# Attention, dense FFN and routed experts in one kernel: how the last two token blocks get their second FFN weight, and which queue asks for the first expert's weights

## The chip, the cores and the metric

The kernel runs on one core of a Trainium2 chip. The metric is the device time of one execution in microseconds (us), lower is better. The kernel before takes 1498.35 us, the median of 3 runs (1492.18 to 1498.37).

## The reference

Three parts follow each other on 4608 tokens of width 512: pooled attention, a dense FFN with a piecewise quadratic activation, and eight routed experts of which each token visits one.

```python
# attention: keys and values averaged over groups of 8 positions
attn = softmax(scale * q @ k_p.T); x = attn @ v_p          # -> [4608, 512]
# dense FFN
h = x @ w_in                                               # [4608, 2048]
g = where(h >= 1, h, where(h <= -1, 0, (h + 1) ** 2 / 4))
x = g @ w_out                                              # w_out [2048, 512]
# routed experts, top 1 of 8
expert = argmax(x @ w_gate); gate = max of softmax
out = gate * (relu(x @ w1[expert]) @ w2[expert])           # w1 [8, 512, 1024], w2 [8, 1024, 512]
```

## The kernel before, in words

Matrix products that need the accuracy are done in three matmuls each: both operands are held as a large part (`hi`, rounded to fp32r) and a rest (`lo`), and hi·hi, hi·lo and lo·hi are added in PSUM. A tensor is split by one Copy on ScalarE (ACT), which writes `hi`, and one subtract on VectorE (DVE), which writes `lo`.

The 36 token tiles of 128 form ten blocks, `BLK = [3, 4, 4, 4, 4, 4, 4, 4, 3, 2]`. The dense FFN is one list of 160 steps `g = 16 * j + m`: block `j`, and chunk `m` of 128 of the 2048 hidden columns. For step g, `f1` makes the hidden chunk (12 matmuls with the block's tokens as columns: 512, 384 or 256) and its activation, and `f2` multiplies it by row chunk m of `w_out` (3 matmuls of 512 columns per token tile). `f1` runs two steps ahead (`AHEAD = 2`): loop turn g issues `f1` of step g + 2, then `f2` of step g, and in two slots between and behind them the attention work for the next block, the routing of the block before and small preparations. Everything is issued in the order in which it is written (a manual schedule), and each engine works through its queue in that order.

The activation of one step is a chain between two engines. DVE clips the PSUM bank (line L535), ACT squares (L536), DVE takes the larger into the bank (L546), ACT copies out the hi part (L547), DVE subtracts to get the lo part (L557). The clipped value lives in one buffer `FR`, the banks `ps[0]` and `ps[1]` alternate, so `f1` of step g + 2 waits for L557 of step g. `f2` of step g reads both parts, and w_out's chunk in `WO[:, g % 4]`.

The split of `w_out` is made once, in block 1: there a chunk comes as fp32 (`load_32`, L509), ACT and DVE split it into `WO` (L512 and the subtract in `low_part`, L233), and the pair of parts is stored to the DRAM buffer `wo_d`. From block 2 on `load_out` (L520) fetches the finished pair from there, 512 KB for each step, requested on ACT's queue right behind L547; it is requested three turns ahead of the `f2` that reads it.

While the last two blocks run, the weights of the expert with the most tokens are fetched too: `load_first(i)`, eight requests of 512 KB into the staging areas `ST1` and `ST2` (in tile `AT`, which the attention has used before), at fixed slots `LF`, on ACT's queue (L761 and L763). At slots of the last block they are split on the chip (`cvt1`, Copy L978), the first tokens of that expert are transposed (`q_tx`, L872 to L876), and `f1e` and `f2e` (L908 to L925) start that expert behind the last block.

Routing of a finished block: DVE transposes its output (L594), PE makes logits (L602, L608), DVE finds places (L620 to L647), SP stores the rows (L648), and POOL scatters the token numbers into `perm_d`, 4 bytes per token, one indirect DMA for each tile (L655). Each scatter waits for the one before. At the end POOL reads a part of the table back (L741), DVE turns it into floats (L747) and PE transposes it (L752).

Of the kernel before, what the change touches and what calls it, by code (L numbers as in the profile page):

```python
# [12 lines left out]
ACTF = mybir.ActivationFunctionType  # L13
# [3 lines left out]
ACT = mybir.EngineType.Activation  # L17
DVE = mybir.EngineType.DVE
POOL = mybir.EngineType.Pool
SP = mybir.EngineType.SP  # L20
# [3 lines left out]
def attention_ffn_routed_experts_kernel(  # L24
# [12 lines left out]
    nc = tc.nc  # L37
# [3 lines left out]
    NE, _, EF = w1.shape  # L41
# [3 lines left out]
    KF = DFF // 128  # L45
# [16 lines left out]
    NB = len(blocks)  # L62
# [7 lines left out]
    w32_d = dram.tile([KF, 128, DM], F32, name="w32_d")  # L70
# [6 lines left out]
    def r32(ap):  # L77
        return ap.bitcast(F32)
# [3 lines left out]
    WO = sb.tile([128, 4, 2, DM], F32R, name="WO")  # L82
# [14 lines left out]
    def at(o, n, p=128):  # L97
        return AT[0:p, o:o + n]

    def fx(o, n):  # L100
        return FX[:, o:o + n]
# [19 lines left out]
    WOF = [fx(512 + 512 * i, 512) for i in range(4)]  # L121
    DFI = [fx(2560 + 512 * i, 512) for i in range(3)]

    EH = fx(512, 1024)
    XG = [fx(2560 + ROW * i, ROW) for i in range(3)] + [fx(2044, ROW)]

    def wi(m, lo, c):
        o = m * 1024 + lo * 512 + c * 128
        return W[:, o:o + 128]
# [49 lines left out]
    FSR = sb.tile([128, 1], I32, name="FSR")  # L179
# [52 lines left out]
    def low_part(lo, x, hi, eng=nc.gpsimd):  # L232
        eng.tensor_tensor(out=lo, in0=x, in1=r32(hi), op=ALU.subtract)  # L233
# [3 lines left out]
    def mix(n=1):  # L237
        for _ in range(min(n, len(pend))):
            pend.popleft()()
# [268 lines left out]
    def load_32(m):  # L508
        nc.scalar.dma_start(out=WOF[m % 4], in_=w32_d[m])  # L509

    def split_out(m):
        nc.scalar.activation(out=WO[:, m % 4, 0], in_=WOF[m % 4], func=ACTF.Copy)  # L512

    def split_low(m):
        low_part(WO[:, m % 4, 1], WOF[m % 4], WO[:, m % 4, 0], nc.vector)
        nc.sync.dma_start(out=r32(wo_d[m]), in_=r32(WO[:, m % 4]))

    def load_out(g):

        nc.scalar.dma_start(out=r32(WO[:, g % 4]), in_=r32(wo_d[g % KF]))  # L520

    def f1(j, m):
        g = j * KF + m
        n = blocks[j][1] * 128
        o = ps[m % 2][:, 0:n]
        for c in range(KD):
            xh, xl = XT[:, j % 2, 0, c, 0:n], XT[:, j % 2, 1, c, 0:n]
            nc.tensor.matmul(o, wi(m, 0, c), xh, start=(c == 0), stop=False)  # L528
            nc.tensor.matmul(o, wi(m, 0, c), xl, start=False, stop=False)  # L529
            nc.tensor.matmul(o, wi(m, 1, c), xh, start=False, stop=(c == KD - 1))  # L530
        r = (JK if j == 0 and m % 2 else FR)[:, 0:n]
        gh, gl = FG[:, g % (AHEAD + 1), 0, 0:n], FG[:, g % (AHEAD + 1), 1, 0:n]


        nc.vector.tensor_scalar(r, o, -1.0, 1.0, op0=ALU.max, op1=ALU.min)  # L535
        nc.scalar.activation(out=r, in_=r, func=ACTF.Square, scale=0.5, bias=half)  # L536
        mix()

        def larger():
            if j == 0:  # L540

                nc.vector.tensor_tensor(out=G32[m % 3], in0=r, in1=o, op=ALU.max)
                if m == KF - 1:
                    load_32(0)
                return
            nc.vector.tensor_tensor(out=o, in0=r, in1=o, op=ALU.max)  # L546
            nc.scalar.activation(out=gh, in_=o, func=ACTF.Copy)  # L547
            if j == 1:
                split_out(m)
                if m + 1 < KF:  # L550
                    load_32(m + 1)
            if g + 1 >= 2 * KF and g + 1 < len(steps):
                load_out(g + 1)
            later.append(lower)

        def lower():
            nc.vector.tensor_tensor(out=gl, in0=o, in1=r32(gh), op=ALU.subtract)  # L557
            if j == 1:
                split_low(m)
        later.append(larger)  # L560

    def f2(j, m):
# [136 lines left out]
    def e1(lo):  # L699
        return W[:, lo * 4096:(lo + 1) * 4096].rearrange("p (c f) -> p c f", c=KD)  # L700
# [4 lines left out]
    ST1 = at(0, 4096).rearrange("p (c f) -> p c f", c=KD)  # L705
    ST2 = at(4096, 4096).rearrange("p (c f) -> p c f", c=KE)
# [47 lines left out]

    def load_first(i):
        if not first:
            first.append(nc.values_load(FSR[0:1, 0:1], engines=[ACT], min_val=0, max_val=NE - 1))
        src = (w1, w2)[i // 4][bass.ds(first[0], 1)].rearrange("o (c p) f -> p (o c) f", p=128)

        if i < 4:  # L760
            nc.scalar.dma_start(out=ST1[:, i:i + 1], in_=src[:, i:i + 1])  # L761
        else:
            nc.scalar.dma_start(out=ST2[:, 2 * i - 8:2 * i - 6], in_=src[:, 2 * i - 8:2 * i - 6])  # L763

    first = []

# [181 lines left out]
    def u_h(j, hf):  # L948
        o = ps[hf]
        x = XR[j % 4]  # L950
        for c in range(KD):
# [4 lines left out]
            nc.tensor.matmul(o, x[:, 1, cs], e1(0)[:, c, fs], start=False, stop=(c == KD - 1))  # L956
        nc.scalar.activation(out=EH[:, hf * 512:(hf + 1) * 512], in_=o, func=ACTF.Relu)

    def u_th(hb, hf, pb):
        for i in range(4):  # L960
            c = 4 * hf + i
            nc.tensor.transpose(pb[:, i * 128:(i + 1) * 128], EH[:, c * 128:(c + 1) * 128],
                                ident)
# [59 lines left out]
    with tc.manual_schedule():  # L1023
# [62 lines left out]
        steps = [(j, m) for j in range(NB) for m in range(KF)]  # L1086
# [14 lines left out]
        def slot(j, s):  # L1101
# [15 lines left out]
            for i in range(8):  # L1117
                if 32 * (j - NB + 2) + s == LF[i]:
                    load_first(i)
# [28 lines left out]
        for m in range(AHEAD):  # L1148
            f1(0, m)
            flush()  # L1150
        for g, (j, m) in enumerate(steps):
# [19 lines left out]
            if g + AHEAD < len(steps):  # L1171
                f1(*steps[g + AHEAD])
            else:
                f1e(0, g + AHEAD - len(steps))
# [192 lines left out]
```

## Time and profile before

| what | before |
|---|---|
| median of 3 runs | 1498.35 us |
| the profiled execution | 1499.88 us, span of its instructions 1497.6 us |
| PE (TensorE matmul) busy | 1441.0 us, 96% of the span |
| DVE, ACT, POOL busy | 789.6, 462.9, 215.1 us (53%, 31%, 14%) |
| moved by DMA | 177.65 MB, mean 119 GB/s |

PE is busy nearly all the time, so a change that leaves its matmuls alone counts by the waits of PE that it removes or makes. Transfers are requested on three queues, ACT's, SP's and POOL's, and run on the same 16 DMA engines. In the rows below, times are us from the start of the span, and the last two blocks run from about 895 to 1035 us. ACTq rows are requests on ACT's queue.

### The profile page before, as it was taken

How to read it: one execution, taken by the hardware profiler on the slowest of the kernel's cores; microseconds unless marked ns; L12 is line 12 of the kernel's file. 1: busy time of each engine (PE TensorE's matmuls, PEld its weight loads, DVE VectorE, ACT ScalarE, POOL GpSimd, SP SyncE). 2: the span in 40 equal slices, each digit the busy share in tenths (PEclk: the TensorE clock that was granted, in tenths of full speed). 3: DMA queues.
4: the chain of work that ended last, by engine and by line, in shares of the span. 5: the costliest groups of instructions: out<-in, count | busy, mean ns of one | idle time of the engine just before them, and what ended most of it. 6: DMA issues, size and time to landing. Idle time of an engine off the chain costs nothing.

```text
span 1497.6 us, 20434 instructions
## 1 busy us (share of the span) xinstructions
PE 1441.0 (96%) x7703; PEld 1165.8 (78%) x7703; DVE 789.6 (53%) x1569; ACT 462.9 (31%) x861; POOL 215.1 (14%) x230
## 2 busy tenths in 40 slices
PE   6899999999999999999999999978999999999997
PEld 5666777778888778788878888867878888888786
DVE  4689887646756655756745546444522222212426
ACT  5344433333333332333333233233111111111324
POOL 3152000001000001010010011002222220111112
PEclk8899999999999999999999999999999999999999
DMA  8575558348458465465374374983331110110414
GB/s 233 165 226 158 179 161 186 104 109 125 126 113 124 122 115 102 141 118 120 120 98 115 103 92 144 155 232 72 112 122 57 57 57 22 43 50 30 140 50 148
DMA packets 106522, 177.65 MB, mean 119 GB/s; under 512 B 48450, under 2 KB 56789, under 8 KB 106400
## 3 DMA queue, kind: packets, MB, share of 16 engines
q10 hardware_dynamic: 22688, 75.77, 24.2%
q1 hardware_dynamic: 76144, 80.00, 19.3%
q0 software_dynamic: 7568, 20.33, 4.3%
q8 instruction: 67, 1.10, 0.4%
q14 instruction: 55, 0.45, 0.1%
HBM read 167.17 MB, written 32.49 MB: 133 GB/s over the span
## 4 chain that ended last, share of the span: by engine, by line
PE 76%; DMA 7%; issue 7%; DVE 7%; ACT 1%; POOL 1%; SPq 1%; ACTq 0%; another core or an unknown queue 0%; POOLq 0%; DVEq 0%
PE ps L528 8%; PE ps L571 8%; PE ps L529 8%; PE ps L530 8%; PE ps L573 7%; PE ps L572 7%; PE ps L908 3%; PE ps L909 3%; PE ps L910 3%; PE ps L923 3%; PE ps L924 3%; PE ps L925 3%; PE ps L357 2%; PE ps L302 2%; PE ps L344 2%
## 5 line engine op out<-in xcount | busy, mean ns | idle before, releaser
L528 PE MATMUL ps<-XT,W 128*128 128x512 f32 (+2 forms) x640 | 250.9, 392 | 0.0
L529 PE MATMUL ps<-XT,W 128*128 128x512 f32 (+2 forms) x640 | 238.1, 372 | 1.6 <-DVE XT L363 1.6
L530 PE MATMUL ps<-XT,W 128*128 128x512 f32 (+2 forms) x640 | 237.7, 371 | 0.0
L571 PE MATMUL ps<-WO,FG 128*128 128x512 f32 x528 | 218.2, 413 | 11.1 <-DMA WO<-wo_d 7.2
L536 ACT ACTIVATE FX<-FX,half 128x512 f32<-128x512 f32 (+2 forms) x152 | 104.0, 684 | 401.7 <-DVE FX L535 398.6
L572 PE MATMUL ps<-WO,FG 128*128 128x512 f32 x528 | 207.8, 394 | 0.0
L573 PE MATMUL ps<-WO,FG 128*128 128x512 f32 x528 | 207.8, 393 | 0.0
L535 DVE TENSOR_SCALAR FX<-ps 128x512 f32<-128x512 f32 (+2 forms) x152 | 96.4, 634 | 156.7 <-PE ps L530 156.5
L914 DVE SCALAR_TENSOR_TENSOR FG<-ps,FG 128x512 fp32r<-128x512 f32 (+1 forms) x64 | 43.2, 674 | 221.3 <-ACT FG L913 221.3
L528 PEld LDWEIGHTS ps<-XT,W 128*128 128x128 f32 x640 | 121.7, 190 | 22.6 <-issue 4.5
L529 PEld LDWEIGHTS ps<-XT,W 128*128 128x128 f32 x640 | 122.0, 191 | 19.0 <-DVE XT L363 2.3
L530 PEld LDWEIGHTS ps<-XT,W 128*128 128x128 f32 x640 | 121.5, 190 | 19.5
L571 PEld LDWEIGHTS ps<-WO,FG 128*128 128x128 f32 x528 | 99.6, 189 | 34.8 <-issue 5.3
L546 DVE TENSOR_TENSOR ps<-FX,ps 128x512 f32<-128x512 f32 (+2 forms) x144 | 92.9, 645 | 55.1 <-ACT FX L536 55.1
L547 ACT ACTIVATE FG<-ps 128x512 fp32r<-128x512 f32 (+2 forms) x144 | 80.9, 562 | 123.6 <-DVE ps L546 113.3
L913 ACT ACTIVATE FG<-ps 128x512 fp32r<-128x512 f32 (+1 forms) x64 | 37.4, 584 | 259.5 <-PE ps L910 258.9
L573 PEld LDWEIGHTS ps<-WO,FG 128*128 128x128 f32 x528 | 99.6, 189 | 22.9
L572 PEld LDWEIGHTS ps<-WO,FG 128*128 128x128 f32 x528 | 99.9, 189 | 17.0
L336 POOL TENSOR_TENSOR AT<-AT,ssm 128x576 f32<-128x576 f32 x36 | 41.4, 1151 | 481.1 <-DVE ssm L329 473.2
L557 DVE TENSOR_TENSOR FG<-ps,FG 128x512 fp32r<-128x512 f32 (+2 forms) x144 | 91.9, 638 | 34.8 <-ACT FG L547 34.4
L923 PE MATMUL ps<-W,FG 128*128 128x512 f32 x248 | 99.2, 400 | 0.0
L908 PE MATMUL ps<-XT,W 128*128 128x512 f32 (+1 forms) x256 | 98.4, 384 | 0.0
(238 smaller groups left out, 2317.9 us busy)
## 6 DMA issues: line engine op xcount, KB each, us to landing
WO<-wo_d ACTq DMA_DIRECT2D x128, 512.0 KB
AT<-in_moe_w_dram SPq DMA_DIRECT2D x10, 2048.0 KB
AT<-in_moe_w_dram SPq DMA_DIRECT2D x14, 1024.0 KB
AT<-in_v_dram SPq DMA_DIRECT2D x60, 144.0 KB
AT<-in_q_dram SPq DMA_DIRECT2D x32, 256.0 KB
wo_d<-WO SPq DMA_DIRECT2D x16, 512.0 KB
AT<-in_k_dram SPq DMA_DIRECT2D x56, 144.0 KB
yrow_d<-Y SPq DMA_DIRECT2D x7, 1032.0 KB
```

Source lines behind the costliest of these rows:

```text
L528: nc.tensor.matmul(o, wi(m, 0, c), xh, start=(c == 0), stop=False)
L529: nc.tensor.matmul(o, wi(m, 0, c), xl, start=False, stop=False)
L530: nc.tensor.matmul(o, wi(m, 1, c), xh, start=False, stop=(c == KD - 1))
L535: nc.vector.tensor_scalar(r, o, -1.0, 1.0, op0=ALU.max, op1=ALU.min)
L536: nc.scalar.activation(out=r, in_=r, func=ACTF.Square, scale=0.5, bias=half)
L546: nc.vector.tensor_tensor(out=o, in0=r, in1=o, op=ALU.max)
L557: nc.vector.tensor_tensor(out=gl, in0=o, in1=r32(gh), op=ALU.subtract)
L571: nc.tensor.matmul(o, gh, WO[:, g % 4, 0], start=(m == 0), stop=False)
L572: nc.tensor.matmul(o, gh, WO[:, g % 4, 1], start=False, stop=False)
L573: nc.tensor.matmul(o, gl, WO[:, g % 4, 0], start=False, stop=(m == KF - 1))
L908: nc.tensor.matmul(o, e1(0)[:, c, ms], xh, start=(c == 0), stop=False)
L923: nc.tensor.matmul(o, gh, e2(0)[:, m], start=(m == 0), stop=False)
```

## The change

Two edits. In the last two blocks (steps 128 to 159, `S0 = 128`) `wo_d` is no longer read. A step's chunk comes as fp32 from `w32_d`, 256 KB, into one of three buffers `WL` in tile `FX`, requested on ACT's queue five turns ahead of its `f2`; two turns later ACT copies the hi part into `WO` and DVE subtracts for the lo part, both behind the activation of the step that is made then. And `load_first` issues on SP's queue instead of ACT's.

```diff
+    WL = [fx(512, 512), fx(1024, 512), fx(2044, 512)]
...
+    S0 = (NB - 2) * KF
+
+    def load_last(g):
+        if S0 <= g < len(steps):
+            nc.scalar.dma_start(out=WL[g % 3], in_=w32_d[g % KF])
+
+    def split_last(g):
+        nc.scalar.activation(out=WO[:, g % 4, 0], in_=WL[g % 3], func=ACTF.Copy)
+
+    def split_last_low(g):
+        low_part(WO[:, g % 4, 1], WL[g % 3], WO[:, g % 4, 0], nc.vector)
...
-            if g + 1 >= 2 * KF and g + 1 < len(steps):
+            if 2 * KF <= g + 1 < S0:
                 load_out(g + 1)
+            load_last(g + 3)
+            if S0 <= g + 1 < len(steps):
+                split_last(g + 1)
             later.append(lower)
...
             nc.vector.tensor_tensor(out=gl, in0=o, in1=r32(gh), op=ALU.subtract)
             if j == 1:
                 split_low(m)
+            if S0 <= g + 1 < len(steps):
+                split_last_low(g + 1)
...
-            first.append(nc.values_load(FSR[0:1, 0:1], engines=[ACT], min_val=0, max_val=NE - 1))
+            first.append(nc.values_load(FSR[0:1, 0:1], engines=[SP], min_val=0, max_val=NE - 1))
...
-            nc.scalar.dma_start(out=ST1[:, i:i + 1], in_=src[:, i:i + 1])
+            nc.sync.dma_start(out=ST1[:, i:i + 1], in_=src[:, i:i + 1])
...
-            nc.scalar.dma_start(out=ST2[:, 2 * i - 8:2 * i - 6], in_=src[:, 2 * i - 8:2 * i - 6])
+            nc.sync.dma_start(out=ST2[:, 2 * i - 8:2 * i - 6], in_=src[:, 2 * i - 8:2 * i - 6])
```

The lines of the changed file stand 13 lower from L536 to L557 (L535 is L548, L536 is L549, L546 is L559, L547 is L560; L557 is L573, 16 lower) and 18 lower behind; L233 is L234.

ACT's queue in the last block, two turns in a row (steps 150 and 151), before; FG is the hidden chunk, FX the tile of the clipped value, AT the staging area, and the DMA rows are requests:

```order
L536 ACTIVATE FX<-FX,half 128x256
L547 ACTIVATE FG<-ps_67 128x256
L520 DMA WO<-wo_d 128x1024
L536 ACTIVATE FX<-FX,half 128x256
L547 ACTIVATE FG<-ps_68 128x256
L520 DMA WO<-wo_d 128x1024
L763 ISA
L763 DMA AT<-in_moe_w_dram 128x2x512
```

The same place of the changed kernel:

```order
L549 ACTIVATE FX<-FX,half 128x256
L560 ACTIVATE FG<-ps_67 128x256
L523 DMA FX<-w_d 128x512
L526 ACTIVATE WO<-FX 128x512
L549 ACTIVATE FX<-FX,half 128x256
L560 ACTIVATE FG<-ps_68 128x256
L523 DMA FX<-w_d 128x512
L526 ACTIVATE WO<-FX 128x512
```

The request is half as large, the expert's request is gone from this queue, and a Copy of 512 columns (L526) stands between L560 of one step and L549 of the next.

DVE's queue over the same two steps, before:

```order
L535 TENSOR_SCALAR FX<-ps_67 128x256
L546 TENSOR_TENSOR ps_67<-FX,ps_67 128x256
L557 TENSOR_TENSOR FG<-ps_67,FG 128x256
L535 TENSOR_SCALAR FX<-ps_68 128x256
L546 TENSOR_TENSOR ps_68<-FX,ps_68 128x256
L557 TENSOR_TENSOR FG<-ps_68,FG 128x256
```

And in the changed kernel:

```order
L548 TENSOR_SCALAR FX<-ps_67 128x256
L559 TENSOR_TENSOR ps_67<-FX,ps_67 128x256
L573 TENSOR_TENSOR FG<-ps_67,FG 128x256
L234 TENSOR_TENSOR WO<-FX,WO 128x512
L548 TENSOR_SCALAR FX<-ps_68 128x256
L559 TENSOR_TENSOR ps_68<-FX,ps_68 128x256
L573 TENSOR_TENSOR FG<-ps_68,FG 128x256
L234 TENSOR_TENSOR WO<-FX,WO 128x512
```

A subtract of 512 columns now stands between the end of one step's activation and the clip of the next.

SP's queue behind the last loads of the attention (q, k, v into AT), before; `yrow_d` is the store of a block's rows, the last three of blocks 7, 8 and 9 among them, and TB the table of the experts' part:

```order
L206 DMA AT<-in_q_dram 128x8x64 x3
L648 DMA yrow_d<-Y 128x4x516 x2
L648 DMA yrow_d<-Y 128x3x516
L648 DMA yrow_d<-Y 128x2x516
L1013 TENSOR_LOAD TB
```

And in the changed kernel, where FSR holds the number of the first expert:

```order
L666 DMA yrow_d<-Y 128x4x516 x2
L775 TENSOR_LOAD FSR
...
L779 DMA AT<-in_moe_w_dram 128x1024
...
L781 DMA AT<-in_moe_w_dram 128x2x512
L781 ISA
L781 DMA AT<-in_moe_w_dram 128x2x512
L666 DMA yrow_d<-Y 128x3x516
L781 ISA
L781 DMA AT<-in_moe_w_dram 128x2x512
L781 ISA
L781 DMA AT<-in_moe_w_dram 128x2x512
L666 DMA yrow_d<-Y 128x2x516
```

The eight requests stand on SP now, six of them directly behind the row store of block 7 and two behind that of block 8.

## Rows read from the trace of the kernel before

**Rows 1.** Two stretches: length; PE, PEld, DVE, ACT, POOL busy (count); PE clock; DMA; GB/s

```profile
895.00:965.00 70.00, 69.87 (x409) 61.15 (x408) 36.99 (x98) 22.26 (x43) 9.00 (x10) 1.00 0.63 135
965.00:1035.00 70.00, 58.29 (x366) 51.07 (x365) 31.20 (x83) 23.48 (x47) 9.02 (x7) 0.95 0.78 196
```

**Rows 2.** Timeline, ACT's queue at the start of the last block (start, us, instruction)

```profile
970.81 4.43 ACTq L761 DMA_DIRECT2D AT<-in_moe_w_dram  x1
975.28 1.09 ACT L580 ACTIVATE Y<-ps 128x512 f32<-128x512 f32 x2 [4.66 <-issue]
```

**Rows 3.** Timeline of PE: waits for w_out (in brackets: idle before, releaser)

```profile
1003.95 0.77 PE L571 MATMUL ps<-WO,FG 128*128 128x512 f32 x1 [4.30 <-DMA WO<-wo_d]
...
1013.02 0.47 PE L571 MATMUL ps<-WO,FG 128*128 128x512 f32 x1 [1.31 <-DMA WO<-wo_d]
...
1026.98 0.47 PE L571 MATMUL ps<-WO,FG 128*128 128x512 f32 x1 [1.59 <-DMA WO<-wo_d]
```

**Rows 4.** Timeline: ACT's requests of two of these three chunks

```profile
998.86 0.33 ACTq L520 DMA_DIRECT2D WO<-wo_d  x1
...
1017.89 0.33 ACTq L520 DMA_DIRECT2D WO<-wo_d  x1
```

**Rows 5.** Timeline of POOL: the first of block 8's three scatters, the table read

```profile
992.61 0.97 POOL L655 DMA_INDIRECT perm_d<-idt,POSI  x1 [27.48 <-DVE SM L646]
...
1023.76 0.90 POOL L741 DMA_INDIRECT FX<-perm_d,RWM  x1 [5.47 <-PE ps L572]
```

**Rows 6.** Timeline: PE's part of one turn, step 155 on f2

```profile
1017.73 0.28 PE L528 MATMUL ps<-XT,W 128*128 128x256 f32 x1
...
1019.16 0.40 PE L571 MATMUL ps<-WO,FG 128*128 128x512 f32 x1
...
1020.55 0.60 PE L872 MATMUL ps<-ident,FX 128*128 128x128 f32 x4
```

**Rows 7.** Timeline: the activation of step 158, to the clip of 159

```profile
1023.16 0.42 DVE L535 TENSOR_SCALAR FX<-ps 128x256 f32<-128x256 f32 x1
...
1023.61 0.51 ACT L536 ACTIVATE FX<-FX,half 128x256 f32<-128x256 f32 x1 [1.15 <-DVE FX L535]
...
1024.15 0.43 DVE L546 TENSOR_TENSOR ps<-FX,ps 128x256 f32<-128x256 f32 x1 [0.58 <-ACT FX L536]
...
1024.62 0.38 ACT L547 ACTIVATE FG<-ps 128x256 fp32r<-128x256 f32 x1 [0.49 <-DVE ps L546]
...
1025.03 0.42 DVE L557 TENSOR_TENSOR FG<-ps,FG 128x256 fp32r<-128x256 f32 x1 [0.45 <-ACT FG L547]
...
1025.43 0.42 DVE L535 TENSOR_SCALAR FX<-ps 128x256 f32<-128x256 f32 x1
```

**Rows 8.** Timeline of block 1, where chunks are split: DVE and ACT

```profile
197.21 0.68 DVE L233 TENSOR_TENSOR WO<-FX,WO 128x512 fp32r<-128x512 f32 x1
...
201.07 0.60 ACT L547 ACTIVATE FG<-ps 128x512 fp32r<-128x512 f32 x1 [0.28 <-DVE ps L546]
...
201.56 0.62 ACT L512 ACTIVATE WO<-FX 128x512 fp32r<-128x512 f32 x1
```

**Rows 9.** The same columns, from the clip of step 146 to that of 159

```profile
972.21:1025.43 53.22, 43.10 (x282) 37.73 (x282) 24.67 (x70) 18.97 (x37) 7.27 (x6) 0.94 0.81 194
```

**Rows 10.** Groups of DVE instructions in that stretch (busy, mean; idle before)

```profile
L233 DVE TENSOR_TENSOR W<-AT,W 128x1024 fp32r<-128x1024 f32 x2 | 2.5, 1226 | 2.3 <-ACT W L978 2.3
L594 DVE STREAM_TRANSPOSE WG<-Y 128x512 f32<-128x512 f32 x3 | 2.1, 699 | 0.0
L875 DVE TENSOR_TENSOR XT<-ps,XT 128x512 fp32r<-128x512 f32 x3 | 2.1, 692 | 1.7 <-ACT XT L874 1.7
```

**Rows 11.** Timeline of PE and DVE behind the last block

```profile
1028.34 0.22 DVE L747 CAST FX<-FX 32x128 f32<-32x128 int32 x1 [0.55 <-DMA FX<-perm_d,RWM]
1028.45 0.34 PE L908 MATMUL ps<-XT,W 128*128 128x384 f32 x1
...
1032.04 0.24 PE L752 MATMUL ps<-ident,FX 32*128 32x32 f32 x1
```

## The prediction

> **What bounds the kernel now.** I looked first at the busy time by stretch. In block 8 PE is busy for 69.87 of 70 us, so nothing can be won there; in block 9 and what borders it for 58.29 of 70, at a mean granted clock of 0.95 [rows 1]. So this change is worth something in the 70 us around block 9, or nowhere. The waits of PE there have two causes. Three are for a chunk of w_out that had not landed: 4.30, 1.31 and 1.59 us, 7.2 together [rows 3]. The fourth is behind ACT's queue: one request for the expert's weights held ACT for 4.43 us, the evacuation of block 8 stood behind it and began 4.66 us late [rows 2], and the next f2 needs the banks that it empties. With the lower clock behind the two long waits, about 13 us of PE time are lost.
>
> Why the chunks are late is seen from request and use. The chunk that PE took at 1013.02 was requested at 998.86, 14.2 us before; that of 1026.98 at 1017.89, 9.1 us before [rows 3, 4]. That is not their size: the whole stretch moves 196 GB/s [rows 1], at which 512 KB take 2.7 us. Over the same time POOL's three scatters follow each other, from 992.61 to the table read at 1023.76, 10.4 us each [rows 5]. The use at 1013.02 and the end of the second scatter, by this count at 1013.4, fall together; that at 1026.98 comes behind the third.
>
> **The change, part by part.**
>
> *Requests moved to SP.* ACT no longer issues eight requests. Seven of them cost it nothing that shows; the long one goes, and with it the wait of 4.66 us and the slow matmuls behind it: about 5 us at the start of block 9, if nothing takes their place. On SP they stand behind the row store of block 7 and wait only for their staging area, which the attention has left by then, so they come up to 30 us earlier than on ACT. Nobody waits for SP there; what is queued behind them is the row store of block 8 and two of the eight, read at the expert's start at the earliest. I price the earlier traffic at nothing beside the landings below.
>
> *Chunks loaded at half size.* 32 requests of 512 KB become 32 of 256 KB. They are made five turns ahead of their f2 instead of three, but their first reader is now ACT's Copy two turns after the request. A chunk that is late now holds ACT's queue, and with it every activation, instead of PE alone.
>
> *The splits.* 32 Copies and 32 subtracts of 512 columns. Block 1 has both: the Copy 0.62 us, 0.49 us after L547 starts; the subtract 0.68 [rows 8]. By busy time they fit: in the last block's stretch DVE works 24.67 of 53.22 us and ACT 18.97 [rows 9], and 13 subtracts are 8.8. But they don't lie in a free place. The activation is one chain over two queues that are worked through in order. From one clip to the next it takes 0.45 (clip to square), 0.54 (to L546), 0.47 (to L547), 0.41 (to L557) and 0.40 (to the next clip), 2.27 us [rows 7]. In the changed order the Copy stands behind L547 and the subtract behind the Copy, and the next clip behind the subtract: 0.45 + 0.54 + 0.47 + 0.49 (L547 to Copy) + 0.65 (Copy and 0.03 of hand-over) + 0.66 (subtract, with the overlap of 0.02 that rows 7 show) = 3.26 us a turn. PE's own turn is 1.43 us for f1 and 1.39 for f2, 2.82 us [rows 6]. So the chain, which had 0.55 us a turn to spare, becomes 0.44 us longer than PE's turn, and the last block is bound by DVE and ACT together, neither of them busy.
>
> In block 8 the same sum does not bite: tokens are 384 columns and the turn of PE is 70 us over some 15 turns, 4.7 us [rows 1], against 3.26 and some 0.15 for each of the four longer instructions; the cover is 0.8 us a turn, which the attention's last units use up for a few turns, and the two steps of lead hold that. I price block 8 at nothing.
>
> *The sum for the last block*, from the clip of step 146 to that of step 159, 13 turns. Before: 972.21 to 1025.43 [rows 9]. After: the start is 0.4 later, because one subtract stands ahead of it (0.66, less a pause there). 13 turns of 3.26 are 42.4. Other DVE work on the chain: 24.67 busy less 13 x 1.27 for the three steps of the activation (0.42 + 0.43 + 0.42 [rows 7]) leaves 8.2; of it two of the three transposes of L594 (0.7 each) and one of the logits (0.3) stand behind L546, where DVE waits anyway, so 6.5; and DVE's waits for ACT's conversions, 2.3 and 1.7 [rows 10], stay: 10.5. The last term is waiting for landings and for PE's logits. It is bounded by zero (256 KB, requested two turns or 6.5 us ahead) and by the landings of rows 3 and 4: one of 14.2 and two of 9.1 against 6.5 are 12.9. The load on the queues falls by half, and a turn with a conversion is over 4 us long, so I take 2.5, nearer to zero. Sum: 972.6 + 42.4 + 10.5 + 2.5 = 1028.0, the clip of step 159 comes 2.6 us later than before.
>
> PE gives that back. Before, it was behind the chain: f1e began at 1028.45 [rows 11], 3.0 us after the last clip, because of the late chunk. After, f1e needs only the bank that L557 of step 158 frees, 1.80 - 0.83 = 0.97 us ahead of the last clip, so at 1027.1. From there on everything follows as before. **The change gains 1028.45 - 1027.1, 1.3 us.** Against the profiled execution's 1499.88 us that is 1498.6; the median of the three runs, 1498.35, is 1.5 lower than that execution, so I forecast 1497.0. What was lost to transfers is lost to the chain instead.
>
> [...]
>
> **The rivals.**
>
> *B, the splits are hidden.* If a turn stays with PE (the Copy and subtract find room, or my 3.26 is too long), all four waits and the slow matmuls go, 13 us. The next limit is then the chain of scatters: the first is issued at 992.61, the table is read and on DVE at 1028.34, and PE transposes it at 1032.04 [rows 5, 11]. The first scatter would move up by the 5 us lost ahead of it, the table to 1023.5, so PE's transpose comes 8 us earlier and not 13: 1490. If scatters go faster with fewer bytes beside them, up to 1486. For it: both engines have idle time. Against it: the order puts both instructions in the one cycle.
>
> *C, late landings on ACT's queue, slower than before.* The waiting term is all that is needed: the chain has 3.9 us to give (1.3 + 2.5) before the change costs time. Three scatters, each catching one request at its middle, give about 2.6 us each by the 9.1 us landing, 7.8 together, and one more for the scatters of block 7 that run into this block, 10.4: a loss of 6.6, 1505. If the 14.2 us come back once, 5 more. For it: the rows above. Against it: half the bytes, and 2 MB of the expert's weights are moved out of this stretch.
>
> *D, neither edit shows*, because PE catches the evacuation late for another reason and landings decide as before: 1498.
>
> **How the numbers follow.** A (the chain takes over, 1.3 us gained, 1493 to 1501 with the bounds of its terms) 0.58; B 0.23; C 0.14; D 0.05. The range that leaves out no more than 2 in 10 runs from B's middle to below C's: 1488.5 to 1504. Half a per cent, 7.5 us, is about what a measurement can tell here, as the three runs of before lie 6 us apart (1492.18 to 1498.37). Faster by more than that is most of B and a little of the rest: 0.20. Slower is a part of C: 0.10. Same: 0.70.
>
> **What the profile after would show.** Right: no wait at the start of block 9 and no request over 1 us on ACT; PE's waits in block 9 many and short, released by DVE and ACT instead of transfers, 8 to 13 us in all; clips at least 3.2 us apart in turns with no other work; the subtract's wait for the Copy in every turn. B: clips 2.8 us apart, and a wait of L747 or L752 for the table. C: waits of L526 for WL of several us. The forecast fails if the split's Copy or subtract is much quicker here than in block 1, or if landings cost over 4 us.

## The result: 0.8% slower

The changed kernel takes 1510.4 us, the median of 5 runs (1508.27 to 1513.28); in the same session the kernel before takes 1498.37 (5 runs). The ratio is 1.0078, 95% interval 1.0053 to 1.0102; timed again later it was 1511.14 us, 1.0083 (1.0058 to 1.0108). The profiled execution took 1508.75 us, its instructions span 1507.0 us (before: 1499.88 and 1497.6). The forecast of 1497.0 us and its range up to 1504 are missed, on the side of rival C. In this text a late chunk is one that ACT or PE stands and waits for, and the times in the lines are read from one execution each.

The two stretches of [rows 1] in the changed kernel, with the same columns:

```profile
895.00:965.00 70.00, 68.61 (x399) 59.77 (x397) 44.59 (x111) 29.07 (x56) 7.92 (x8) 1.00 0.57 125
965.00:1035.00 70.00, 54.77 (x338) 47.39 (x337) 40.41 (x91) 29.44 (x56) 10.47 (x8) 0.90 0.42 82
```

The last column is in line with the edits: 82 GB/s in place of 196 around block 9. But PE is busy 3.5 us less there, its granted clock fell from 0.95 to 0.90, and block 8, which had no gap, has one. Where PE, ACT and DVE stood (table of waits: engine, line waited for, releaser; us in total, times, longest; PE from 890 to 1130 us, ACT and DVE to 1050):

```profile
PE ps L541 <- DVE FG L573: 10.4, 4, 4.6
...
ACT WO L526 <- DMA FX<-w_d: 9.1, 5, 3.8
...
DVE WO L234 <- ACT WO L526: 11.3, 13, 4.0
```

PE no longer waits for a transfer: the waits of [rows 3] are gone. The transfers are waited for by ACT, at the Copy of the split (L526), 9.1 us in five waits; DVE waits for ACT, and PE for DVE. This is the sign that the forecast gave for C. The first long one, at the start of block 9, in the timeline:

```profile
962.00 0.33 ACTq L523 DMA_DIRECT2D FX<-w_d  x1
...
967.18 1.10 POOL L673 DMA_INDIRECT perm_d<-idt,POSI  x1 [7.81 <-DMA perm_d<-idt,POSI]
...
973.10 0.63 ACT L526 ACTIVATE WO<-FX 128x512 fp32r<-128x512 f32 x1 [3.77 <-DMA FX<-w_d]
...
976.93 1.07 ACT L598 ACTIVATE Y<-ps 128x512 f32<-128x512 f32 x2
...
977.57 0.50 PE L589 MATMUL ps<-WO,FG 128*128 128x512 f32 x1 [3.98 <-ACT Y L598]
...
978.27 0.41 DVE L548 TENSOR_SCALAR FX<-ps 128x256 f32<-128x256 f32 x1
```

The last scatter of block 7 goes out at 967.18; ACT stands 3.77 us for a chunk that was requested at 962.00, 11.1 us earlier; the evacuation L598 is behind it in the same queue, and PE waits for that 3.98 us (3.8 before). So the 4.66 us of [rows 2] were not removed but exchanged: a chunk in place of a request, on the same queue, in front of the same instruction.

A turn without any other work, DVE and ACT:

```profile
999.59 0.42 DVE L548 TENSOR_SCALAR FX<-ps 128x256 f32<-128x256 f32 x1
1000.04 0.51 ACT L549 ACTIVATE FX<-FX,half 128x256 f32<-128x256 f32 x1 [1.09 <-DVE FX L548]
1000.59 0.43 DVE L559 TENSOR_TENSOR ps<-FX,ps 128x256 f32<-128x256 f32 x1 [0.58 <-ACT FX L549]
1001.11 0.38 ACT L560 ACTIVATE FG<-ps 128x256 fp32r<-128x256 f32 x1 [0.56 <-DVE ps L559]
...
1001.53 0.43 DVE L573 TENSOR_TENSOR FG<-ps,FG 128x256 fp32r<-128x256 f32 x1 [0.51 <-ACT FG L560]
1001.56 0.63 ACT L526 ACTIVATE WO<-FX 128x512 fp32r<-128x512 f32 x1
...
1002.23 0.69 DVE L234 TENSOR_TENSOR WO<-FX,WO 128x512 fp32r<-128x512 f32 x1 [0.27 <-ACT WO L526]
1002.83 0.42 DVE L548 TENSOR_SCALAR FX<-ps 128x256 f32<-128x256 f32 x1
```

From clip to clip 3.24 us, step by step as the forecast put it together from [rows 7, 8]; it said 3.26. The next turn, and what follows from it. The first row is the request of the chunk that is late in it; the last two are the start of f1e and the clip of step 159, which were at 1028.45 and 1025.43 before:

```profile
997.88 0.33 ACTq L523 DMA_DIRECT2D FX<-w_d  x1
...
1007.56 0.63 ACT L526 ACTIVATE WO<-FX 128x512 fp32r<-128x512 f32 x1 [2.82 <-DMA FX<-w_d]
...
1012.72 0.44 PE L541 MATMUL ps<-XT,W 128*128 128x256 f32 x1 [3.96 <-DVE FG L573]
...
1016.18 3.38 DVE L234 TENSOR_TENSOR WO<-FX,WO 128x512 fp32r<-128x512 f32 x1 [0.27 <-ACT WO L526]
...
1016.59 2.41 POOL L234 TENSOR_TENSOR W<-AT,W 128x1024 fp32r<-128x1024 f32 x1
...
1025.24 0.58 PE L541 MATMUL ps<-XT,W 128*128 128x256 f32 x1 [4.65 <-DVE FG L573]
...
1036.49 0.44 PE L926 MATMUL ps<-XT,W 128*128 128x384 f32 x1
...
1037.14 0.42 DVE L548 TENSOR_SCALAR FX<-ps 128x256 f32<-128x256 f32 x1
```

ACT stands 2.82 us for a chunk requested 9.7 us earlier, and PE, which has no turn in hand any more, 3.96 us. Right behind it something comes that the forecast did not know: a subtract of the split lasts 3.38 us in place of 0.69, beside a POOL subtract that makes a part of the expert's weights, and PE waits another 4.65 us. Behind these waits PE's clock is lower for a while: 0.50 is granted from 1013 to 1016, and 0.80 on the mean from 1005 to 1030. f1e begins 8.0 us later than before, and the span ends 9.4 later.

### The profile page after: what moved, and what is told of

Same layout as the page of the kernel before. It is cut to its first block, busy times and chain, and to the rows that moved or that the text cites. A ratio compares the mean times of both kernels' runs of the same rounds, so it can differ in the third digit from the quotient of the medians.

```text
span 1507.0 us, 20498 instructions
## 1 busy us (share of the span) xinstructions
PE 1443.4 (96%) x7703; PEld 1166.4 (77%) x7703; DVE 812.3 (54%) x1601; ACT 481.0 (32%) x893; POOL 215.1 (14%) x230
## 5 line engine op out<-in xcount | busy, mean ns | idle before, releaser
L541 PE MATMUL ps<-XT,W 128*128 128x512 f32 (+2 forms) x640 | 252.7, 395 | 10.5 <-DVE FG L573 10.4
L549 ACT ACTIVATE FX<-FX,half 128x512 f32<-128x512 f32 (+2 forms) x152 | 104.0, 684 | 393.7 <-DVE FX L548 393.4
L548 DVE TENSOR_SCALAR FX<-ps 128x512 f32<-128x512 f32 (+2 forms) x152 | 96.3, 633 | 137.3 <-PE ps L543 137.2
L541 PEld LDWEIGHTS ps<-XT,W 128*128 128x128 f32 x640 | 122.8, 192 | 34.9 <-DVE FG L573 12.5
L543 PEld LDWEIGHTS ps<-XT,W 128*128 128x128 f32 x640 | 123.0, 192 | 19.6
L542 PEld LDWEIGHTS ps<-XT,W 128*128 128x128 f32 x640 | 123.2, 192 | 18.8 <-DVE XT L364 2.3
L559 DVE TENSOR_TENSOR ps<-FX,ps 128x512 f32<-128x512 f32 (+2 forms) x144 | 92.9, 645 | 51.5 <-ACT FX L549 51.5
L560 ACT ACTIVATE FG<-ps 128x512 fp32r<-128x512 f32 (+2 forms) x144 | 81.0, 562 | 122.7 <-DVE ps L559 111.2
L573 DVE TENSOR_TENSOR FG<-ps,FG 128x512 fp32r<-128x512 f32 (+2 forms) x144 | 91.9, 638 | 35.0 <-ACT FG L560 34.6
```

## The experiments

Three theories to begin with. **Theory 1**: late fp32 chunks hold ACT's queue. **Theory 2**: the split lengthens the chain of DVE and ACT beyond PE's turn. **Theory 3**: the expert's traffic, which SP starts earlier, is what makes the chunks late.

### Each edit alone

The requests on SP alone (the last three lines of the diff):

> Only the requests for the first expert's weights are moved to SP; w_out still comes as finished pairs from wo_d. If the move is harmless by itself, the long request on ACT and the 4.66 us wait at the start of block 9 are gone, the waits of PE for w_out chunks (7.2 us before) stay, and the time is 1493 to 1498 us. If the earlier expert traffic is what makes the chunks late (theory 3), the waits of PE for w_out grow to over 12 us, some of them in block 8, and the time is 1500 us or more. No wait of block 9 is released by ACT or DVE for several us, as there are no splits.

1505.26 us, ratio 1.0031 (1.0014 to 1.0049): slower, where the forecast priced this edit as a gain of 5 if nothing took its place. Waits of PE, and one of them in the timeline:

```profile
PE ps L571 <- DMA WO<-wo_d: 12.6, 5, 5.6
```

```profile
957.11 0.76 PE L571 MATMUL ps<-WO,FG 128*128 128x512 f32 x1 [4.46 <-DMA WO<-wo_d]
```

The wait behind the evacuation is gone, but 12.6 us for w_out stand against 7.2, and 4.46 of them in block 8, which had none. Theory 3 is right for this kernel.

The loads and splits alone, the requests on ACT:

> Only the loads as fp32 and the splits; the expert's requests stay on ACT's queue. Theory 1 (late fp32 chunks hold ACT's queue) and theory 2 (the split lengthens the chain of DVE and ACT) both give 1508 to 1516 us, since the cause is all here and the long request of some 4 us on ACT comes back. Theory 3 (the traffic that SP starts earlier makes the chunks late): the waits of L526 fall from 9.1 us to under 3 and the time is within 1496 to 1503 us.

1502.63 us, ratio 1.0030 (1.0010 to 1.0049). In the table of waits:

```profile
ACT WO L526 <- DMA FX<-w_d: 3.2, 4, 1.4
```

3.2 us in place of 9.1 (12.1 when the changed kernel was profiled again, below), just by leaving the expert's requests where they were. Theories 1 and 2, as far as they put the whole loss into this edit, are refuted. By the ratios each edit costs about 4.5 us and both together 11.7; the intervals don't show whether that is more than the sum.

### Only the time of the expert's requests, not their queue

```diff
+    def gate(g):
+        nc.sync.dma_start(out=gate_d, in_=r32(FG[0:1, g % (AHEAD + 1), 1, 0:16]))
...
                 if 32 * (j - NB + 2) + s == LF[i]:
+                    gate(j * KF + s // 2 + 1)
                     load_first(i)
```

> The changed kernel, with the expert's requests still on SP's queue but each behind a 64-byte store on that queue that reads the hidden chunk of the step being made, so that they go out at the steps at which ACT issued them before, and not up to 30 us earlier. If it is the early traffic that makes the chunks late, the waits of L526 fall from 9.1 us to about the 3.2 of the run with the requests on ACT, and the time is 1499 to 1504 us. If SP's queue itself does it, whatever the time, the waits stay at 7 us or more and the time at 1507 or more.

1503.70 us, ratio 1.0041 (1.0029 to 1.0054); L526 waits 3.2 us in six waits, the longest 1.5. So the queue does no harm to the chunks; it is the time of the requests. In the changed kernel SP asks for six times 512 KB right behind the row store of block 7, within some 10 us:

```profile
936.88 2.78 SPq L779 DMA_DIRECT2D AT<-in_moe_w_dram  x4
939.86 5.71 SPq L781 DMA_DIRECT2D AT<-in_moe_w_dram  x2
```

The same hold on the kernel before, with w_out as pairs:

> The kernel before with the expert's requests on SP's queue, held there to the steps at which ACT issued them; w_out as pairs. If the early traffic was the whole harm of the move to SP, PE's waits for w_out go from the 12.6 us of the run without the hold back to the 7 of before, the 4.66 us behind ACT's long request stay away, and the time is 1493 to 1497 us. If not, PE still waits 10 us or more for w_out and the time is 1499 us or more: then the long request cost nothing that was to be had.

1503.10 us, ratio 1.0017 (1.0001 to 1.0033). PE waits 8.9 us for w_out, between the two cases; the time is that of the second, nothing is gained. The long request on ACT is gone, and in the same place PE now waits for a late chunk:

```profile
978.29 0.77 PE L572 MATMUL ps<-WO,FG 128*128 128x512 f32 x1 [3.42 <-DMA WO<-wo_d]
```

That the 4.66 us had covered it before is an inference. What this run shows is the requests on another queue, at the same steps, and no gain (1.0017).

### One turn more of lead

```diff
-    WL = [fx(512, 512), fx(1024, 512), fx(2044, 512)]
+    WL = [fx(512, 512), fx(1024, 512), fx(2044, 512), WG[:, 5]]
...
-            load_last(g + 3)
+            load_last(g + 4)
```

> The changed kernel with four WL buffers in place of three, the fourth in tile WG, so that each fp32 chunk is requested one turn (3.2 us in block 9, 4.7 in block 8) earlier. Theory 1: the waits of L526 fall from 9.1 us to under 2, the evacuation behind block 8 is on time, and of the 12 us lost 6 to 9 come back: 1501 to 1504 us. Theory 2: turns stay at 3.25 us, PE waits in every turn of block 9, and no more than the 3 us of the two long waits beyond the chain come back: 1506 to 1509 us.

1500.45 us, ratio 1.0008 (0.9994 to 1.0022). Waits, and the clips of steps 146 and 159 in the timeline:

```profile
ACT WO L526 <- DMA FX<-w_d: 1.8, 1, 1.8
```

```profile
975.87 0.41 DVE L548 TENSOR_SCALAR FX<-ps 128x256 f32<-128x256 f32 x1
...
1030.69 0.42 DVE L548 TENSOR_SCALAR FX<-ps 128x256 f32<-128x256 f32 x1
```

Theory 1: the lead gives back about 10 us of the changed kernel's loss (1.0078 to 1.0008). Some 2.7 of them may be luck, as no subtract of the split is stretched in block 9 in this execution. The chain is unchanged here, and from clip 146 to 159 it takes 54.8 us.

### The subtract behind the next clip

In f1, where DVE waits for ACT's square anyway; the chain no longer has the subtract in it:

```diff
         nc.vector.tensor_scalar(r, o, -1.0, 1.0, op0=ALU.max, op1=ALU.min)
+        if S0 <= g:
+            split_last_low(g)
...
         def lower():
-            if S0 <= g + 1 < len(steps):
-                split_last_low(g + 1)
```

> The changed kernel, with the subtract of a chunk's split moved on DVE from in front of the next clip to behind it, where DVE waits for ACT's square; loads and their lead are as they were. Theory 2: undisturbed turns of block 9 fall from 3.25 us to PE's 2.82 or so, 13 turns give back 5.6 us, with the lower clock that went with PE's waits 6 to 9: 1501 to 1504 us, the L526 waits as they were or longer. Theory 1: PE's waits go on to follow the late chunks (L526 waits 8 to 12 us, since a shorter turn also shortens the lead), 1507 to 1510 us.

1502.45 us, ratio 1.0008 (0.9988 to 1.0028). Waits:

```profile
ACT WO L526 <- DMA FX<-w_d: 12.4, 8, 5.1
```

Theory 2 has its part too: ACT stands for chunks as long as in the changed kernel or longer (12.4 us; 9.1 and 12.1 in that one's two profiles), and yet most of the loss is gone. The reading is that the chain catches up between the waits.

### Both mends

> Both mends at once: four WL buffers (requests one turn earlier) and the subtract behind the next clip. Each alone gave back 8 to 10 of the 12 us. If late chunks and the long chain are two losses that add up, L526 waits under 3 us in all, turns of block 9 come to 2.8 to 2.9 us, PE's waits in block 9 fall under 4 us, and the time is 1490 to 1495 us, faster than before. If they are one loss that either mend removes (a late chunk costs only while the chain has no slack), the time is 1498 to 1501 us.

1493.80 us, ratio 0.9968 (0.9952 to 0.9983): faster than both kernels. Most of the two gains adds up: by the ratios 16.5 us against the changed kernel, where each mend alone gave about 10. A turn in its timeline, from clip to clip:

```profile
991.87 0.41 DVE L548 TENSOR_SCALAR FX<-ps 128x256 f32<-128x256 f32 x1
...
992.23 0.69 DVE L234 TENSOR_TENSOR WO<-WG,WO 128x512 fp32r<-128x512 f32 x1
992.32 0.51 ACT L551 ACTIVATE FX<-FX,half 128x256 f32<-128x256 f32 x1
...
994.14 0.41 DVE L548 TENSOR_SCALAR FX<-ps 128x256 f32<-128x256 f32 x1
...
1021.68 0.33 PE L926 MATMUL ps<-XT,W 128*128 128x384 f32 x1
```

The subtract L234 runs beside the square, and the turn can go down to 2.27 us, the length before the change, which is less than PE's 2.82. The turns are not all 2.8 to 2.9 us as expected: the 13 from clip 146 to 159 take 46.2 us together, against 53.2 before and 58.9 in the changed kernel. f1e begins at 1021.68, 6.8 us earlier than before. L526 waited 3.7 us in this execution, a little more than expected, all of it in block 8, where the chain has room for it.

Two variants of it, with the expert's requests held to the steps of before, and with all eight of them in block 8:

> Both mends (four WL buffers, subtract behind the next clip) and the expert's requests on SP held to the steps of before. If early expert traffic costs anything beyond the lead of the chunks, this is 2 to 4 us faster than the same kernel without the hold; if a turn more of lead covers it, the two agree within 2 us. By the forecast's case B it is 1488 to 1494 us.

> Four WL buffers, the subtract behind the next clip, and all eight expert requests in block 8. If a turn more of lead covers the traffic in block 8 too, this is 0 to 3 us faster than the same kernel with two requests in block 9 (1493.8 us), 1490 to 1494. If the bunch in block 8 gets too large for the lead, L526 waits over 6 us there and the time is 1495 to 1500 us.

1494.68 us, ratio 0.9970 (0.9959 to 0.9982), and 1494.06 us, 0.9957 (0.9941 to 0.9974). The three agree: with a turn more of lead and the subtract moved, it doesn't matter where the traffic lies.

### POOL's subtract beside the split's

The two subtracts of the first expert's weights that POOL makes in block 9 are given to DVE (two, not the four that the expectation names); on the changed kernel, on the one with both mends, and the changed kernel once more beside them:

```diff
-        low_part(e1(1)[:, c], ST1[:, c], e1(0)[:, c], nc.gpsimd if c % 2 else nc.vector)
+        low_part(e1(1)[:, c], ST1[:, c], e1(0)[:, c], nc.vector)
```

> The changed kernel with the first expert's four subtracts on POOL (2.4 us each) made by DVE, where they take 1.23 us. If POOL's instruction is what stretches DVE's subtracts with two operands in SBUF, no subtract of the split lasts over 0.75 us any more, the turn from clip 154 to 155 falls from 6.59 us to 5.2 or less (one subtract of 1.23 may lie in it), and the time is 0 to 3 us less than the changed kernel's, since DVE now has 1.23 us more in two turns of the block. If something else stretches them (the lower clock behind a wait, a landing), the turn stays over 6 us or another subtract is stretched, and the time is 1 to 4 us more.

> The kernel with four WL buffers and the subtract behind the next clip, and the same move from POOL to DVE. If POOL's instruction stretches DVE's, no subtract of the split lasts over 0.75 us; the time is within 2 us of the 1493.8 of the same kernel without the move, since its chain has the room for one stretched subtract. If the stretch cost it anything near 3 us, the time is 1489 to 1491.

> The changed kernel once more, nothing edited: 1508 to 1512 us, ratio 1.006 to 1.010.

1512.17 us, ratio 1.0096 (1.0073 to 1.0119); 1492.76, 0.9968 (0.9955 to 0.9982); 1511.14, 1.0083 (1.0058 to 1.0108). Timed again, the changed kernel once more has a stretched subtract of 3.26 us, and the turn from clip 154 to 155 lasts 6.49 us (6.59 the first time). Without POOL's two, no subtract of the split lasts over 0.69 us from 940 us on, and this turn is 3.90. So POOL's instruction is the cause; but the time did not fall as expected. DVE's 1.23 us now lie in the chain in other turns (that from 153 to 154 is 4.72 us in place of 3.24), and the 13 turns last 59.1 us. With both mends the time is the same with and without the move. That it is not the number of columns shows in the kernel with both mends, at a subtract of 16 columns of the routing:

```profile
1040.61 2.39 POOL L234 TENSOR_TENSOR W<-AT,W 128x1024 fp32r<-128x1024 f32 x1 [8.88 <-ACT W L1001]
...
1040.64 2.39 DVE L659 TENSOR_TENSOR G<-G,ebase 128x16 f32<-128x16 f32 x1
```

It starts 0.03 us behind POOL's and ends with it (1043.03 and 1043.00). The subtract of 3.38 us starts 0.41 us ahead of POOL's by the profile and ends 0.56 us behind it. Why a DVE instruction lasts longer beside POOL's is not shown.

### What holds a chunk: traffic, row store or scatter

All eight expert requests ahead of block 8's row store, so that block 9 has no such traffic:

```diff
-    LF, CV1, QT0 = (24, 26, 28, 30, 33, 36, 39, 42), (13, 15, 18, 21), (17, 20, 23)
+    LF, CV1, QT0 = (24, 26, 28, 30, 33, 36, 37, 38), (13, 15, 18, 21), (17, 20, 23)
```

> The changed kernel with the last two of the expert's eight requests moved in the program ahead of block 8's row store on SP, so that all eight go out in block 8 and none beside the first scatter of block 9. If the bunched expert traffic is what makes a chunk late, the wait of L526 at about 1007 us (2.82 us) falls under 0.5 us and those in block 8 and at its end (6.3 us) grow by 1 to 4. If a scatter in flight is enough, the wait in block 9 stays at 2 us or more. Time 1504 to 1511 us either way.

1507.99 us, ratio 1.0056 (1.0034 to 1.0078). In the timeline:

```profile
997.04 0.97 POOL L673 DMA_INDIRECT perm_d<-idt,POSI  x1 [26.11 <-DVE SM L664]
997.31 0.37 SPq L666 DMA_DIRECT2D yrow_d<-Y  x1
...
1007.60 0.63 ACT L526 ACTIVATE WO<-FX 128x512 fp32r<-128x512 f32 x1 [2.08 <-DMA FX<-w_d]
```

The wait stays at 2.08 us without the traffic. The waits ahead of it, which were expected to grow by 1 to 4 us, are 6.3 us in sum as before; the longest in block 8 is 4.70 us, against 1.48 and 4.01 in the two profiles of the changed kernel. But the row store is requested 0.27 us after the scatter and is a rival to it. Three kernels look at that, all with this order of the expert's requests, in one execution each, so that their rows are read and not their times. Moving the scatters in the program by twelve steps of the routing's list:

> The kernel with all eight expert requests in block 8, and block 8's three scatters issued three turns later (first at about 1007 us in place of 997), with the table read behind them moved too; the row store of block 8 stays at about 997. If a scatter in flight is what holds a chunk's landing, there is no wait of L526 over 0.5 us between 995 us and the first scatter, and one of 1.5 us or more within 10 us behind it. If the row store (774 KB) beside the chunks does it, the wait of 2.08 us stays at about 1007. The table read comes some 10 us later, so the time is not compared.

It told nothing: POOL had nothing to do in between and issued the first scatter at 996.36 all the same; the wait (1.88 us) stood at 1006.74. To hold the scatters, they were then made to read their places from a copy that DVE writes at that step; and in the other kernel the row store was put behind a 64-byte store of the hidden chunk, on SP:

> All eight expert requests in block 8, and block 8's scatters held back some three turns by letting them read their places from a copy that DVE makes at that step; the row store stays at about 997 us. If the scatter in flight holds the landings, no wait of L526 over 0.5 us stands between 995 us and the first scatter, and one of 1.5 us or more stands within 10 us behind it. If the row store does it, the wait of about 2 us stays at 1005 to 1009 us. The table read comes later by as much, so the time is not compared.

> All eight expert requests in block 8, the scatters where they were (first at about 997 us), and the row store of block 8 held back on SP's queue until some five turns later. If the scatter in flight holds the landings, the wait of L526 at 1005 to 1009 us stays at 1.5 us or more. If the row store does it, that wait falls under 0.5 us and one may stand where the row store goes now.

With the scatters held:

```profile
1004.09 0.37 SPq L666 DMA_DIRECT2D yrow_d<-Y  x1
...
1014.08 1.97 POOL L675 DMA_INDIRECT perm_d<-idt,WG  x1 [38.37 <-DVE WG L685]
...
1026.25 0.63 ACT L526 ACTIVATE WO<-FX 128x512 fp32r<-128x512 f32 x1 [2.14 <-DMA FX<-w_d]
```

The DMA engines in two stretches of that execution (columns as in [rows 1]):

```profile
1014.08:1025.00 10.92, 8.87 (x54) 7.10 (x52) 6.30 (x13) 5.38 (x10) 3.88 (x3) 1.00 0.70 24
1025.00:1027.00 2.00, 0.00 (x0) 0.00 (x0) 0.00 (x0) 0.75 (x2) 1.41 (x1) 1.00 0.74 263
```

And with the row store held:

```profile
998.62 0.97 POOL L678 DMA_INDIRECT perm_d<-idt,POSI  x1 [27.46 <-DVE SM L670]
...
1004.75 0.38 SPq L649 DMA_DIRECT2D yrow_d<-Y  x1
...
1009.13 0.63 ACT L527 ACTIVATE WO<-FX 128x512 fp32r<-128x512 f32 x1 [2.02 <-DMA FX<-w_d]
```

The wait goes with the scatter. With the scatters held, the turns of 3.24 us beside the row store pass without a wait of L526, and one of 2.14 us comes behind the first scatter (12 us behind it, not within 10 as expected). With the row store held, the wait is the same, 2.02 us, 10.5 us behind the scatter. In that kernel the row store still goes out 4.4 us before the late chunk is there, so it is the first of the two that rules the row store out: there the late chunk comes 22 us behind it.

The stretches show more. Three chunks were requested in the first one, at 1016.66, 1019.90 and 1023.72, and 24 GB/s were moved in it, with the DMA engines 0.70 busy; in the next 2 us 263 GB/s were, about the size of two chunks. So the bytes themselves came late. It is not so that nothing moves beside a scatter: in the changed kernel 185 GB/s were moved from its first in block 9 to the next (996.23 to 1006.55), and the chunk was late all the same.

Two more scatters into a table that nobody reads, on the changed kernel:

> The changed kernel with two more scatters of 128 token numbers each, into a table that nobody reads, issued at about 975 us and 985 us, a stretch in which the changed kernel has no scatter in flight and no wait of L526. If a scatter holds back the landings of other transfers (the forecast's case C), waits of L526 of 2 us or more appear between 975 and 997 us. If the late landings come from the expert's traffic alone, none over 0.5 us appears there. The scatters of block 8 come later for the extra work on POOL's queue, and the end with them, so only the waits are compared.

Undecided by its own terms. The DVE copy that starts them came at 986.84, 12 us later than meant, and the turns there are over 4 us long, so that the lead covered the first. What followed was not predicted, and the row store and two of the expert's requests were on their way beside it: the second added scatter (995.63) stood beside block 8's first (998.75), the next scatter did not go out before 1014.68, and a chunk was there 1.0 us later, 8.44 us late:

```profile
1014.68 0.97 POOL L674 DMA_INDIRECT perm_d<-idt,POSI  x1 [14.96 <-DMA perm_d<-idt,POSI]
1015.69 0.63 ACT L527 ACTIVATE WO<-FX 128x512 fp32r<-128x512 f32 x1 [8.44 <-DMA FX<-w_d]
```

## Why the prediction was wrong

**The chain: right.** The turn is 3.24 us (forecast 3.26). From clip 146 to 159 the 13 turns take 58.9 us; without what the late chunk adds (2.8: a turn of 7.48 us in place of the 4.72 of the run with more lead) and what the stretched subtract adds (2.7: 6.59 in place of 3.90) that is 53.4, where the forecast had 42.4 + 10.5 = 52.9. Right too was that f1e would start ahead of the last clip (by 0.65 us, forecast 0.97), and that the change would exchange one bound for another.

**The step that failed first: "I take 2.5, nearer to zero".** The waiting for landings was sized near the bound of bytes and mean rate. The load did fall (82 GB/s for 196), but the late chunks of 256 KB took 11.1 and 9.7 us from request to use, as those of 512 KB had (14.2 and 9.1). ACT stood 9.1 us, and one turn more of lead gives back about 10 us of the time. The forecast's own sign of failing, landings that cost over 4 us, came. Three things were left out of the term. A wait that the chain can't catch up is passed on in full: that of 2.82 us made its turn 7.48 us in place of 4.72. The term looked at block 9 alone, and 6.3 of the 9.1 us lie ahead of clip 146, where the forecast has nothing for it. And a new subtract lies in the chain, and beside one of POOL's conversions it lasted 3.38 us in place of 0.69, which made the turn from clip 154 to 155 6.59 us in place of 3.90.

**"I price the earlier traffic at nothing": wrong.** The forecast saw that the requests go out up to 30 us earlier, and asked who waits for SP. The ones who pay are the chunks in flight beside them: L526 waited 9.1 and 12.1 us in two profiles with the early requests, 3.2 with the same requests held.

**"About 5 us at the start of block 9, if nothing takes its place": something did.** A late chunk stood behind the request, in the changed kernel (3.77 us) as in the kernel with pairs (3.42). The forecast had the condition and did not look at which chunk was due.

**"I price block 8 at nothing": wrong by about 2 us.** The clip of step 141 comes at 954.89, against 952.99 before. The forecast let the two steps of lead hold a few long turns, and they did not. In the changed kernel PE waits for a small copy of the routing (L622), which stands on ACT behind L560 and the Copy L526:

```profile
917.88 0.62 ACT L526 ACTIVATE WO<-FX 128x512 fp32r<-128x512 f32 x1
...
918.72 0.49 PE L626 MATMUL ps<-WG 128*128 128x128 f32 x2 [1.40 <-ACT WG L622]
```

PE does not wait there in the kernel before. With the subtract behind the next clip, and the Copy where it was, the same wait is shorter (from that kernel's table of waits):

```profile
PE ps L626 <- ACT WG L622: 0.4, 1, 0.4
```

So the Copy in front makes up some 0.4 us of it and the chain, lengthened by the subtracts turn by turn, the other 1.0. The evacuation is alike: with the extra lead alone PE still waits 1.45 us for it; with both mends, and the Copy in the same place, it does not wait.

Together: clip 146 is 6.1 us later than before (1.9 by step 141, 3.5 in the turn with the 3.77 us wait, 0.7 in the others), where the forecast had 0.4; the 13 turns last 58.9 in place of 55.4 (2.8 for the late chunk, where 2.5 stood for all waiting, 2.7 for the stretched subtract, and 0.5 besides); the clip of step 159 comes at 1037.14, 9.1 later than forecast.

**The rivals.** C had the mechanism, the place (ACT's queue, scatters) and the sign; its 1505 was low because it had neither the earlier traffic nor the stretched subtract. B's worth is reached by half: with both causes mended the time is 1493.8, between B's 1490 and the 1498.7 that the kernel before takes in that session.

C has each scatter catch a request. The held runs show a chunk late behind a scatter, at 2.0 to 2.1 us of wait, and in the one with the scatters held the bytes themselves came late (24 GB/s, then 263); the reason is not shown. Nor do a chunk and a scatter end together in the kernel before, as the forecast had it from the mean of 10.4 us: the third scatter goes out at 1014.57, 1.5 us behind the use at 1013.02.

**Open.** The kernel with requests held has only 3.2 us of late chunks and still costs 0.4%, 3 to 5 us more than the one with the longer lead, by the medians and by the ratios (1.0041 and 1.0008); the profile of one execution does not say where these lie. Why a chunk is late behind a scatter stays open too.

## What to carry to other kernels

A load that is moved from the engine that needs it to a queue of its own must have its deadline checked against what is in flight then, not against its size: here it was late behind scatters of 4-byte pieces (2.0 to 2.1 us) and beside a burst of other requests (9.1 us of waits, 3.2 with the same requests held), and one buffer more was worth about 10 us. Extra work on two engines that pass one chain back and forth made an undisturbed turn here 3.24 us, and it belongs where its engine waits for the other: the same subtract, moved behind the next clip, leaves that turn at the 2.27 us of before. And a wait that is to be removed should be looked at for what is late behind it, before it is counted as a gain.

## What was not expected of the hardware

Behind scatters of 128 numbers of 4 bytes, 256 KB that were requested two turns ahead missed their reader by 1.88 to 2.14 us, in four kernels that have no traffic of the expert there; in one of them the DMA engines moved 24 GB/s in the 11 us from the scatter on, with three chunks requested. With two more scatters a chunk was 8.44 us late. And a subtract of 16 columns on DVE lasted 2.39 us, as long as POOL's instruction beside it.
